# Second norm of an adaLN block: statistics and roots ahead of rests, and the second layer's first weight sums and splits issued sooner

## The chip, the cores and the metric

The kernel runs on one core of a Trainium2 chip. A core has five engines, each with an instruction queue of its own that it works through in order: TensorE (PE; its weight loads are listed as PEld), VectorE (DVE), ScalarE (ACT), GpSimd (POOL) and SyncE (SP), which issues most DMA transfers. They meet only through semaphores. SBUF is the working memory, PSUM the memory that TensorE writes its results to. The metric is the device time of one execution in microseconds (us), the median of several runs.

## The reference

The reference is one block of a network on 2048 tokens x 640 channels, fp32, with two halves that are modulated by a condition vector `c`:

```
mod = silu(c) @ w_mod                        # six rows of 640: sa, ca, ga, sb, cb, gb
h = layernorm(x) * (1 + ca) + sa             # x is A_q
x = x + ga * A(h, k, v, shift_k, ssm_k, ssm_D)   # short conv on k, times v, long FFT conv, gate by h
h = layernorm(x) * (1 + cb) + sb
x = x + gb * B(h, w1, b1, w2, b2)
# B: h2 = layernorm(h) over channels (2048 x 640)
#    u = gelu(h2^T w1 + b1)   (640 x 1728; the sum runs over the 2048 tokens)
#    y = u w2 + b2            (640 x 2048), returned as 2048 x 640
```

Between the halves stand two layernorms in a row: the one of the block ("first norm", its result times 1 + cb plus sb) and the one inside B ("second norm"). The change touches the stretch in which they are computed, and the beginning of the product with w2 ("second layer").

## The kernel before, in words

Tokens lie in 16 row blocks j = 0 to 15 of 128 tokens x 640 channels. Every fp32 product is made of three matmuls of a reduced fp32 form: a weight is split into a high part (a rounded copy, made by ScalarE) and a low part (the difference, made by VectorE), the data into a "half" (high) and a "rest" (low), and high x high, high x low and low x high are added in PSUM.

The long convolution of the first half ends with `gate` and the statistics of the new x. Then the program, written out by hand in one fixed order for all engines, works through the row blocks in **pairs** (pair pr holds blocks 2 pr and 2 pr + 1), each pair passing these steps:

- `x1_stats` (VectorE): a piece of statistics and their aggregation for each block; they are made for a pair some passes ahead.
- `root_in(n)`: one or two small POOL operations (lines 737 and 740) that add the epsilon to the variances of the second norm of one pair (their sums come from ScalarE's squares) and of the first norm of a later pair (from `x1_stats`), then ScalarE's square root (line 741). `root(n)` (VectorE) makes the reciprocal roots from them, in a Newton step of four small operations and a fifth for the first norm.
- `norm1` (ScalarE, line 755): the first norm of a pair. `second` (VectorE, lines 761 to 766): the modulation, with the sum for the mean of the second norm, and the subtraction of the mean; ScalarE squares the result (line 771) with a running sum.
- `halves` (ScalarE, line 775): the normalized block, rounded. `rests` (VectorE, line 779): what the rounding left.
- `products`: the matmuls of the pair with the first four blocks of w1 (f = 0 to 3), 48 in number, accumulated in four PSUM banks `acc[0..3]` over all pairs. Of a pair, 32 need the halves and the low parts of the weights, and 16 the rests. For the last pair, 7, they go block by block.
- `split_rows(r, ...)`: the split of the w1 rows of pairs 2 r and 2 r + 1 for these four blocks: four high parts on ScalarE (line 420) and four low parts on VectorE.

The loop over pr = 3 to 7 (second, rests of the pair before, products of the pair before, and so on) stands at the end of this stretch. Roots n = pr + 1 belong to the second norm of pair pr, since the lists in `roots` are one ahead; `root(pr + 1)` has to come before `halves(pr)`, and `rests(pr)` follows in the next pass. `load_w(4)`, in SP's queue, reloads the tile X once its rows have been split.

When the last pair's first block of products is done, the tile of the first weight block is free, `split_w(4)` fills it, and `u_evac` applies gelu to `acc[0..3]`; then come the other blocks of w1 (line 445), a half block (line 919) and the first four columns of w2 (line 1123), kept in `acc[0..3]` again.

The other 12 columns of w2 are multiplied by a scheme that needs seven products instead of eight for a 2 x 2 arrangement of blocks (line 1046). Six pairs p of columns, seven products each, make products n = 0 to 41, in the order A11, A12, S1, S2, S3, S4, A22; S1 to S4 are sums and differences of weight blocks, made by VectorE in `sums(n)`: S1 in sums(2), S2 and S3 in sums(3), S4 in sums(5), all others empty; so for every pair. `split(n)` makes the high part on ScalarE (line 1034) and the low part on VectorE, in one of three slots, n % 3, so that it has to wait for product(n - 3). `product(n)` is 21 matmuls. `outcome(n)` reads its result from PSUM; where an output block is complete, `finish` adds the bias, multiplies by the gate row, adds x and starts the transfer out. Products 0 and 1 share a PSUM tile, and so do 2 and 3; product 4 takes the bank of `acc[2]`, product 5 that of `acc[3]`, which hold columns 2 and 3 of w2 until four calls of `finish` (k = 0 to 3) have read them. `x_pair` loads the x rows for the finishes of a pair of columns.

Of the kernel before, what the change touches and what calls it, by code (L numbers as in the profile page):

```python
# [47 lines left out]
def mixer_kernel(ctx: ExitStack, tc: tile.TileContext, q, k, v, shift_k, ssm_k, ssm_D, w1, b1, w2, b2, c,  # L48
# [11 lines left out]
    def mem(tag, n, name=None):  # L60

        return sb.tile([128, n], F32, name=name or tag, tag=tag, bufs=1)
# [14 lines left out]
    T_in, P, X, T_aux, T_kt = mem("in", 4288), mem("p", 2048), mem("x", 2048), mem("aux", 4096), mem("kt", 1536)  # L77
# [339 lines left out]
    def split_rows(r, t, blocks, hi=True, lo=True):  # L417
        j, t = slice(4 * r, 4 * r + 4), t.rearrange("p (j m) -> p j m", j=4)
        for f in blocks if hi else ():
            act.activation(blk[f][0][:, j].bitcast(F32R), t[:, :, 128 * f:128 * f + 128], AF.Copy)  # L420
        for f in blocks if lo else ():
            TT(dve, blk[f][1][:, j].bitcast(F32R), t[:, :, 128 * f:128 * f + 128], blk[f][0][:, j], ALU.subtract)
# [291 lines left out]
    def x1_stats(js):  # L714
        for j in js:
            x1s(NC - 1, j)()
            dve.bn_aggr(mv[:, j, :], bst[:, j])
# [14 lines left out]
    def root_in(n):  # L732

        second_, first_ = roots[n]
        o = start[n]
        if second_:
            pool.tensor_scalar(V_[:, o:o + 2], V_[:, o:o + 2], 1 / D, EPS, op0=ALU.mult, op1=ALU.add)
            o += 2
        if first_:
            pool.tensor_scalar(V_[:, o:start[n + 1]], mv[:, first_[0]:first_[-1] + 1, 1], EPS, None, op0=ALU.add)  # L740
        act.activation(T_[:, start[n]:start[n + 1]], V_[:, start[n]:start[n + 1]], AF.Sqrt)

    def root(n):

        o = slice(start[n], start[n + 1])
        newton(R_[:, o], T_[:, o], V_[:, o])
        first_ = roots[n][1]
        if first_:
            f = slice(first_[0], first_[-1] + 1)
            dve.scalar_tensor_tensor(nm1[:, f], mv[:, f, 0], -1.0, R_[:, start[n + 1] - len(first_):start[n + 1]],  # L750
                                     op0=ALU.mult, op1=ALU.mult)
# [5 lines left out]
    def second(pr):  # L757

        for j in (2 * pr, 2 * pr + 1):
            t = row(j)  # L760
            dve.scalar_tensor_tensor(t, t, 1.0, CB, op0=ALU.mult, op1=ALU.mult, accum_out=su[:, j:j + 1])
        n = su[:, 2 * pr:2 * pr + 2]
        dve.tensor_scalar(n, n, msb, -1 / D, op0=ALU.add, op1=ALU.mult)
        for j in (2 * pr, 2 * pr + 1):
            t = row(j)
            dve.scalar_tensor_tensor(t, t, su[:, j:j + 1], SB, op0=ALU.add, op1=ALU.add)
        for j in (2 * pr, 2 * pr + 1):
            if j == 12:
                H.extend(unit(mem("xa", 5120, "h_x"), 4))
            H[j] = H[j][:, 0:640], H[j][:, 640:1280]  # L770
            act.activation(H[j][1].bitcast(F32R), row(j), AF.Square, accum_out=at(V_, 2, j))

    def halves(pr):
        for j in (2 * pr, 2 * pr + 1):
            act.activation(H[j][0].bitcast(F32R), row(j), AF.Identity, scale=at(R_, 2, j))

    def rests(pr):
        for j in (2 * pr, 2 * pr + 1):
            dve.scalar_tensor_tensor(H[j][1].bitcast(F32R), row(j), at(R_, 2, j), H[j][0], op0=ALU.mult,
                                     op1=ALU.subtract)  # L780

    def products(pr, fs=range(4)):
        for f_ in fs:
            if f_ == len(acc):
                acc.append(psum().rearrange("p (h m) -> p h m", h=2))
        js = [(f_, j) for j in (2 * pr, 2 * pr + 1) for f_ in fs]
        if pr == 7:
            for f_, j in sorted(js):
                mm(acc[f_], blk[f_][0][:, j], blk[f_][1][:, j], *H[j], False, j == 15)
            return  # L790
        for rest in range(2):
            for f_, j in js:
                wh, wl = blk[f_][0][:, j], blk[f_][1][:, j]
                mm(acc[f_], wh, wl, *H[j], j == 0 and not rest, False, ((wh, H[j][1]),) if rest else
                   ((wh, H[j][0]), (wl, H[j][0])))
# [47 lines left out]
    products(2)  # L843
    for pr in range(3, 8):
        second(pr)
        if pr > 3:
            rests(pr - 1)
            products(pr - 1)
        if pr in (4, 6):
            split_rows(pr // 2, X if pr == 4 else P, range(4), False, True)  # L850
        if pr < 6:
            x1_stats(range(2 * pr + 4, 2 * pr + 6))
        root_in(pr + 1)
        root(pr + 1)
        halves(pr)
        if pr < 6:
            norm1(pr + 2)
        if pr in (3, 5):
            split_rows(pr // 2 + 1, X if pr == 3 else P, range(4), True, False)
        if pr == 4:  # L860
            load_w(4)
    rests(7)
# [148 lines left out]
    def sums(n):  # L1011

        p, w_ = n // 7, ORDER[n % 7]
        if p >= NP:
            return
        a = lambda k: A[p, k]
        if w_ == "S1":
            A[p, w_] = S1
            TT(dve, S1, a("A21"), a("A22"), ALU.add)
        elif w_ == "S2":  # L1020
            TT(dve, a("A21"), a("A11"), a("A21"), ALU.subtract)
            TT(dve, a("A11"), S1, a("A11"), ALU.subtract)
            A[p, "S3"], A[p, "S2"] = a("A21"), a("A11")
        elif w_ == "S4":
            TT(dve, a("A12"), a("A12"), a("S2"), ALU.subtract)
            A[p, "S4"] = a("A12")

    def split(n):

        p, w_ = n // 7, ORDER[n % 7]  # L1030
        if p >= NP:
            return
        W[n] = slots[n % 3]
        act.activation(W[n][0].bitcast(F32R), A[p, w_], AF.Copy)  # L1034
        TT(dve, W[n][1].bitcast(F32R), A[p, w_], W[n][0], ALU.subtract)
# [24 lines left out]
    def outcome(n):  # L1060

        p, w_ = n // 7, ORDER[n % 7]
        t, s, x = bank.pop(n), NW + 2 * p, xq[4 * (p % 2):4 * (p % 2) + 4]
        if w_ == "A11":
            act.activation(p1, t, AF.Copy)
        elif w_ == "S1":
            act.activation(p5, t, AF.Copy)
        elif w_ == "A12":
            finish(s, 0, t, o1, x[0], p1)
        elif w_ == "S2":  # L1070
            TT(dve, u2, t, p1, ALU.add)
        elif w_ == "S3":
            TT(dve, u3, t, u2, ALU.add)
            TT(dve, u2, u2, p5, ALU.add)
            finish(s + 1, 1, u3, o4, x[3], p5)
            if p == NP - 1:
                TT(dve, u3, u3, GB[:, 0:320], ALU.mult)
                TT(dve, u3, u3, x[2], ALU.add)
        elif w_ == "S4":
            finish(s, 1, t, o2, x[1], u2)  # L1080
        elif p == NP - 1:
            finish(s + 1, 0, t, o3, u3)
        else:
            finish(s + 1, 0, t, o3, x[2], u3)
# [16 lines left out]
    for s in range(NW):  # L1101
        i = NF + s
        acc.append(psum().rearrange("p (h m) -> p h m", h=2))
        split_w(i)
        load_w(i + 1)
        if s < 3:
            t_ops(3 + s)
        if s > 1:
            early(s - 2)
        if s == 3:  # L1110
            load_pair(1, 0, 3)
            m_w.append(mem("w1", 4096, "m_w0"))
            slots += [(q7(m_w[0], 1792 * i), q7(m_w[0], 1792 * i + 896)) for i in range(2)]
            split(0)
            split(1)
            sums(2)
            sums(3)
        wh, wl = blk[i]
        for f_ in range(NF):
            u = U[f_]  # L1120
            for k, (w, r) in enumerate(((wh, 0), (wh, 2), (wl, 0))):
                for h in range(2):
                    pe.matmul(acc[s][:, h, 0:320], w[:, f_].bitcast(F32R), u[r + h].bitcast(F32R),  # L1123
                              start=f_ == 0 and k == 0, stop=f_ == NF - 1 and k == 2)
# [9 lines left out]
    t_ops(6, pool)  # L1134
    load_pair(1, 3, 4)
    for n in range(7 * NP):
        if n:
            sums(n + 3)
        split(n + 2)
        product(n)  # L1140
        if n == 1 or n == 3:
            outcome(n - 1)
        if n != 0 and n != 2:
            outcome(n)
        if n == 1:
            for k in range(4):
                finish(2 + k // 2, k % 2, acc[2 + k // 2][:, k % 2, 0:320], (o2, o4, o3, o1)[k], xq[4 + k])
        if n == 2:
            x_pair(1)
        if n % 7 == 6:  # L1150
            load_pair(n // 7 + 2)
            x_pair(n // 7 + 2)
# [34 lines left out]
```

## Time and profile before

| | |
|---|---|
| Time, three runs | 678.05, 681.95, 681.57 us (median 681.57) |
| Profiled execution | 683.93 us, span from first to last instruction 682.1 us |
| Mean granted TensorE clock over the span | 0.975 |
| Busy share of the span | PE 92%, PEld 88%, DVE 73%, ACT 44%, POOL 20% |
| VectorE's waits in the pair loop | ahead of the roots, 0.32 to 0.69 us each |

How to read it: a busy time counts every moment in which the engine had an instruction under way, so a busy TensorE need not be at its peak; matmuls of one shape follow each other in half of the duration that a row gives for one. In a row of a timeline stand the start, the duration of the group, the engine, the line of the program, the operation, output and inputs by the program's names, the shapes, the count, and in brackets the idle time ahead of it with what ended it. In a group of several instructions the duration runs from the first start to the last end. Instructions of VectorE and ScalarE overlap by some 0.08 us, so the distance of two starts is a little less than a duration. L57 is the line of a helper for elementwise operations of two tensors. The granted clock is the share of TensorE's full clock that it was given.

### The profile page before, as it was taken

To read this page: it belongs to the slowest core of one execution; us is meant where nothing else is said; L and a number is where in the kernel's file an instruction comes from. 1 tells how busy PE (TensorE), PEld (TensorE's weight loads), DVE (VectorE), ACT (ScalarE), POOL (GpSimd) and SP (SyncE) were. 2 spreads that over 40 slices of the span, in tenths; PEclk is the share of its full clock that TensorE was granted. 3 is DMA by queue.
4 is the path that set the end of the run, shared out by engine and by line. 5 is a ranking of instruction groups with operands and counts; after the bars stand their busy time and mean duration, and the time that the engine had idled before them with its cause. 6 is when DMAs were issued, how large, how long until landed. Compare 5 with 4: busy or idle time off the path is not lost.

```text
span 682.1 us, 20757 instructions
## 1 busy us (share of the span) xinstructions
PE 629.4 (92%) x9119; PEld 598.4 (88%) x9119; DVE 498.3 (73%) x869; ACT 300.2 (44%) x483; POOL 133.9 (20%) x157
## 2 busy tenths in 40 slices
PE   6878778999999898798899999999999989999997
PEld 2877568899989897688899889999999989999997
DVE  7789589989898279798866622321689779888995
ACT  1654655646657265457654222322344133333331
POOL 6762067226134142000000000000000520000000
PEclk9998989999999799888899999999999999999999
DMA  9999797375426153440308333335441634355601
GB/s 188 219 260 274 246 179 157 91 138 121 66 65 215 35 134 104 91 97 1 62 1 154 62 63 63 62 64 115 120 136 55 197 114 124 102 167 166 184 32 38
DMA packets 166538, 81.23 MB, mean 119 GB/s; under 512 B 90830, under 2 KB 156912, under 8 KB 166448
## 3 DMA queue, kind: packets, MB, share of 16 engines
q1 hardware_dynamic: 159276, 78.32, 47.5%
q10 hardware_dynamic: 6916, 1.31, 1.1%
q8 instruction: 71, 1.16, 0.7%
q0 software_dynamic: 256, 0.28, 0.2%
q14 instruction: 19, 0.16, 0.1%
HBM read 69.40 MB, written 10.49 MB: 117 GB/s over the span
## 4 chain that ended last, share of the span: by engine, by line
PE 68%; DVE 14%; ACT 6%; DMA 5%; issue 3%; SPq 2%; POOL 1%; ACTq 0%; POOLq 0%; DVEq 0%
PE pst L445 20%; PE pst L1046 17%; PE pst L1123 7%; PE pst L223 7%; PE pst L242 6%; PE pst L271 5%; PE pst L291 3%; DVE p L57 3%; ACT z L280 2%; DMA in<-in_w_mod_dram 1%; PE pst L919 1%; DVE tap L57 1%; DMA y<-in_A_ssm_k_dram 1%; DVE sm L548 1%; DVE kt L57 1%
## 5 line engine op out<-in xcount | busy, mean ns | idle before, releaser
L242 PE MATMUL pst<-z,w 128*64 128x64 f32 x2560 | 78.4, 223 | 13.1 <-DVE p L57 6.7
L242 PEld LDWEIGHTS pst<-z,w 128*64 128x64 f32 x2560 | 76.4, 138 | 15.6 <-issue 9.1
L229 ACT ACTIVATE z<-pst 128x1024 f32<-128x1024 f32 (+2 forms) x45 | 43.1, 977 | 46.3 <-PE pst L223 46.2
L57 POOL TENSOR_TENSOR y<-p 128x256 f32<-128x256 f32 x72 | 51.3, 741 | 42.4 <-DVE p L57 42.1
L57 DVE TENSOR_TENSOR p<-pst,kt 128x512 f32<-128x512 f32 x80 | 50.7, 680 | 7.9 <-ACT kt L246 7.9
L1046 PE MATMUL pst<-r_z,m_w 128*128 128x320 f32 x222 | 42.0, 312 | 2.2 <-DVE m_w L57 2.2
L882 ACT ACTIVATE pst<-pst,sm 128x640 f32<-128x640 f32 x13 | 10.0, 767 | 75.9 <-PE pst L445 75.9
L271 PEld LDWEIGHTS pst<-v,y 32*128 32x128 f32 x1280 | 38.2, 187 | 5.4 <-issue 4.8
L271 PE MATMUL pst<-v,y 32*128 32x64 f32 x1280 | 40.1, 272 | 2.5 <-issue 2.3
L246 ACT ACTIVATE kt<-pst 128x512 f32<-128x512 f32 x40 | 24.0, 599 | 34.6 <-PE pst L242 18.7
L1034 ACT ACTIVATE m_w<-m_v 128x896 fp32r<-128x896 f32 x24 | 22.7, 951 | 36.9 <-PE pst L1046 16.8
L223 PE MATMUL pst<-v,x 128*64 128x128 f32 x512 | 34.6, 291 | 4.5 <-issue 4.0
L223 PE MATMUL pst<-v,p 128*64 128x128 f32 x640 | 36.7, 274 | 0.8 <-ACT p L168 0.8
L1046 PEld LDWEIGHTS pst<-r_z,m_w 128*128 128x128 f32 x222 | 35.2, 190 | 2.4 <-DVE m_w L57 2.4
L57 POOL TENSOR_TENSOR m_p<-u_i,r_z 128x320 f32<-128x320 f32 x1 | 0.9, 875 | 183.4 <-issue 183.4
L223 PEld LDWEIGHTS pst<-v,p 128*64 128x64 f32 x640 | 34.8, 137 | 2.1 <-ACT p L168 1.7
L57 DVE TENSOR_TENSOR tap<-tap,kt 128x512 f32<-128x512 f32 x51 | 35.5, 696 | 1.3
L223 PEld LDWEIGHTS pst<-v,x 128*64 128x64 f32 x512 | 31.1, 147 | 5.8 <-issue 5.2
L291 PEld LDWEIGHTS pst<-z,v 64*64 64x64 f32 x1280 | 23.9, 156 | 9.1 <-issue 3.8
L280 ACT ACTIVATE z<-pst 128x512 f32<-128x512 f32 x38 | 20.9, 647 | 23.3 <-PE pst L271 23.3
L291 PE MATMUL pst<-z,v 64*64 64x64 f32 x1280 | 25.3, 241 | 6.3 <-issue 2.4
L57 DVE TENSOR_TENSOR kt<-in,tap 128x512 f32<-128x512 f32 x42 | 28.8, 685 | 1.2
(308 smaller groups left out, 1507.4 us busy)
## 6 DMA issues: line engine op xcount, KB each, us to landing
x<-in_B_w_dram SPq DMA_DIRECT2D x20, 512.0 KB
m_x<-xs SPq DMA_DIRECT2D x28, 160.0 KB
out_dram<-m_x SPq DMA_DIRECT2D x28, 160.0 KB
aux<-in_A_ssm_k_dram SPq DMA_DIRECT2D x8, 512.0 KB
m_v<-in_B_w_dram SPq DMA_DIRECT2D x9, 448.0 KB
in<-in_w_mod_dram SPq DMA_DIRECT2D x4, 960.0 KB
x<-in_B_w_dram SPq DMA_DIRECT2D x7, 448.0 KB
in<-in_A_v_dram SPq DMA_DIRECT2D x22, 128.0 KB
```

The source lines that it names most:

```text
L57: TT = lambda eng, o, a, b, op: eng.tensor_tensor(o, a, b, op=op)
L223: pe.matmul(ps[64 * ri:64 * ri + 64, o:o + 255:2], lhs, F1[:, 128 * ri:128 * ri + 128], start=True, stop=True)
L229: act.activation(Z[:, side, t, :, k0:k1], ps.rearrange("p (a k e) -> p a k e", a=4, e=2)[:, :, k0:k1], AF.Copy)
L242: pe.matmul(ps[64 * h:64 * h + 64, o:o + 64], W2[k1 // 32][:, 2 * (k1 % 32) + ri], rhs, start=True, stop=True)
L246: act.activation(kt.rearrange("p (m i) -> p m i", i=32), pv[:, :, 1], AF.Copy)
L271: pe.matmul(pp[qd // 2][:, o:o + 64], Y[p, ri, i:i + 2].rearrange("p i k -> p (i k)"), V2[p, 64 * ri:64 * ri + 64], start=ri == 0, stop=ri ...
L280: act.activation(o, i, AF.Copy)
L291: pe.matmul(ps[64 * b:64 * b + 64, 512 * e + 64 * jj:512 * e + 64 * jj + 64], V1[p, ri, n2], T2[p, :, 32 * ri + n2], start=ri == 0, stop=r ...
L445: pe.matmul(ps[0:m, h, 0:320], w_.bitcast(F32R), r_[:, 320 * h:320 * h + 320].bitcast(F32R), start=first and i == 0, stop=last and i == 2)
L1034: act.activation(W[n][0].bitcast(F32R), A[p, w_], AF.Copy)
L1046: pe.matmul(bank[n], w[:, i].bitcast(F32R), r.bitcast(F32R), start=i == 0 and k == 0, stop=i == 6 and k == 2)
L1123: pe.matmul(acc[s][:, h, 0:320], w[:, f_].bitcast(F32R), u[r + h].bitcast(F32R), start=f_ == 0 and k == 0, stop=f_ == NF - 1 and k == 2)
```

## The change

In the pair loop, `x1_stats` and `root_in(pr + 1)` stand right behind `second(pr)`, ahead of `rests(pr - 1)` and its products; before, the rests came first. The split of the w1 rows r = 2 and r = 3 is done as a whole in passes 4 and 6: its high parts stand between `root_in` and `root` (before, at the end of passes 3 and 5), its low parts behind the root, the halves and `norm1` (before, behind the products, ahead of the statistics).

In the second layer, sums(5) (S4 of the first pair) is issued ahead of all fast products, split(4) behind outcome(0) and ahead of outcome(1), split(5) behind product(2), and the four finishes are parted: two behind outcome(1), two behind split(5). From n = 4 on the order is as before.

```diff
     for pr in range(3, 8):
         second(pr)
+        if pr < 6:
+            x1_stats(range(2 * pr + 4, 2 * pr + 6))
+        root_in(pr + 1)
         if pr > 3:
             rests(pr - 1)
             products(pr - 1)
         if pr in (4, 6):
-            split_rows(pr // 2, X if pr == 4 else P, range(4), False, True)
-        if pr < 6:
-            x1_stats(range(2 * pr + 4, 2 * pr + 6))
-        root_in(pr + 1)
+            split_rows(pr // 2, X if pr == 4 else P, range(4), True, False)
         root(pr + 1)
         halves(pr)
         if pr < 6:
             norm1(pr + 2)
-        if pr in (3, 5):
-            split_rows(pr // 2 + 1, X if pr == 3 else P, range(4), True, False)
+        if pr in (4, 6):
+            split_rows(pr // 2, X if pr == 4 else P, range(4), False, True)
         if pr == 4:
             load_w(4)
...
             split(0)
             split(1)
-            sums(2)
-            sums(3)
+            for n in (2, 3, 5):
+                sums(n)
...
     for n in range(7 * NP):
-        if n:
+        if n > 2:
             sums(n + 3)
-        split(n + 2)
+        if n not in (2, 3):
+            split(n + 2)
         product(n)
         if n == 1 or n == 3:
             outcome(n - 1)
+        if n == 1:
+            split(4)
         if n != 0 and n != 2:
             outcome(n)
-        if n == 1:
-            for k in range(4):
+        if n == 2:
+            split(5)
+        if n in (1, 2):
+            for k in (2 * n - 2, 2 * n - 1):
                 finish(2 + k // 2, k % 2, acc[2 + k // 2][:, k % 2, 0:320], (o2, o4, o3, o1)[k], xq[4 + k])
         if n == 2:
             x_pair(1)
```

## The prediction

> **What bounds the kernel now.** I read the page first, then the chain that ended last, then the orders of the engines around the two places that the diff touches: the second norm (about 310 to 359 us) and the start of the second layer's fast products (about 541 to 577 us). The page says that TensorE is the bound on the whole, and that VectorE is the second engine of the chain:
>
> ```profile
> span 682.1 us, 20757 instructions
> ...
> PE 629.4 (92%) x9119; PEld 598.4 (88%) x9119; DVE 498.3 (73%) x869; ACT 300.2 (44%) x483; POOL 133.9 (20%) x157
> ...
> PE 68%; DVE 14%; ACT 6%; DMA 5%; issue 3%; SPq 2%; POOL 1%; ACTq 0%; POOLq 0%; DVEq 0%
> ```
>
> A change is therefore worth what it takes from TensorE's idle time, and from the half clock that follows such idle time. The price of one matmul comes from the longest piece of the chain, 98.75/672 = 0.147 us at full clock:
>
> ```profile
> 396.52 98.75 PE pst L445 x672
> ```
>
> TensorE's order shows what it waits for in the second norm (rows of line 445):
>
> ```profile
> 317.62 7.25 PE L445 MATMUL pst<-h_a,wb 128*128 128x320 f32 x48
> 327.62 4.09 PE L445 MATMUL pst<-h_a,wb 128*128 128x320 f32 x16 [2.75 <-ACT h_a L775]
> ...
> 344.10 14.34 PE L445 MATMUL pst<-h_x,wb 128*128 128x320 f32 x96 [0.61 <-ACT h_x L775]
> ```
>
> The 48 matmuls of products(3) end at 324.87; products(4) wait 2.75 us for halves(4), products(6) 0.61 us for halves(6). At the start of the second layer's fast part:
>
> ```profile
> 553.66 1.04 PE L1046 MATMUL pst<-r_z,m_w 128*128 128x320 f32 x6
> ...
> 556.74 0.45 PE L1046 MATMUL pst<-r_z,m_w 128*128 128x320 f32 x2
> 559.36 0.43 PE L1046 MATMUL pst<-r_z,m_w 128*128 128x320 f32 x1 [2.17 <-DVE m_w L57]
> ...
> 569.96 1.04 PE L1046 MATMUL pst<-u_t,m_w 128*128 128x320 f32 x6
> ```
>
> product(3) runs from 553.66, product(4) from 556.74 does two matmuls with its high parts and then waits 2.17 us for VectorE's low part; product(7) begins at 569.96. The windows give the clock right behind that wait and later:
>
> ```profile
> 561.00:562.00 1.00, 1.00 (x6) 1.00 (x5) 0.89 (x1) 0.00 (x0) 0.00 (x0) 0.50 0.29 100
> ...
> 570.00:575.00 5.00, 5.00 (x36) 5.00 (x36) 4.90 (x8) 1.60 (x3) 0.00 (x0) 1.00 0.28 87
> ```
>
> The column behind the five engines is the granted clock: 0.50, then 1.00. Products 4 to 6 are 63 matmuls, 63 x 0.147 = 9.26 us; they took 569.96 - 556.74 = 13.22. So 3.96 us are lost here: 2.17 of waiting and 1.79 of half clock.
>
> **Part B, the second layer's first sums and splits (the larger part).** VectorE's order there, and ScalarE's two high splits:
>
> ```profile
> 540.01 1.65 DVE L57 TENSOR_TENSOR m_v<-m_p,m_v 128x896 f32<-128x896 f32 x1
> 548.91 1.24 DVE L57 TENSOR_TENSOR m_w<-m_p,m_w 128x896 fp32r<-128x896 f32 x1 [7.26 <-ACT m_w L1034]
> 550.08 1.76 DVE L57 TENSOR_TENSOR m_w<-m_v,m_w 128x896 fp32r<-128x896 f32 x1
> 551.76 0.54 DVE L1055 SCALAR_TENSOR_TENSOR m_x<-pst,sm,m_x 128x320 f32<-128x320 f32 x1
> ...
> 553.27 0.55 DVE L1053 SCALAR_TENSOR_TENSOR m_x<-pst,sm,rows 128x320 f32<-128x320 f32 x1
> ...
> 557.22 1.08 DVE L57 TENSOR_TENSOR m_v<-m_v 128x896 f32<-128x896 f32 x1
> 558.22 2.27 DVE L57 TENSOR_TENSOR m_w<-m_v,m_w 128x896 fp32r<-128x896 f32 x2
> ...
> 564.00 0.49 DVE L57 TENSOR_TENSOR m_x<-pst,m_x 128x320 f32<-128x320 f32 x1 [2.11 <-PE pst L1046]
> ...
> 574.61 1.08 DVE L57 TENSOR_TENSOR m_w<-m_p,m_w 128x896 fp32r<-128x896 f32 x1
> ```
> ```profile
> 551.12 0.94 ACT L1034 ACTIVATE m_w<-m_v 128x896 fp32r<-128x896 f32 x1
> 558.42 0.95 ACT L1034 ACTIVATE m_w<-m_v 128x896 fp32r<-128x896 f32 x1 [6.36 <-DVE m_v L57]
> ```
>
> Before, split(4)'s low part (558.22) stands behind outcome(1) (551.76 to 553.27, 1.51 us), four finishes (553.27 to 557.22, 3.95 us, 0.99 each) and sums(5) (557.22, 1.08).
>
> - sums(5) moves into the idle stretch of 7.26 us that ends at 548.91. It costs 1.08 to 1.65 us there (the row at 540.01 is the same operation, slowed) and nothing on the path; its cover is wide.
> - split(4)'s low part can start once split(3)'s has ended (550.08 + 1.76 = 551.84) and its high part is there (551.12 + 0.94 = 552.06): 552.1 to 553.1. product(4) then finds it 3.6 us ahead of 556.74, so the 2.17 go, and with the idle time the half clock, 1.79.
> - What is late next? VectorE goes on with outcome(1) to 554.6, two finishes to 556.6, split(5)'s low part to 557.6 (its high part is free once product(2) has left its slot, at 553.66), two finishes to 559.6, outcome(3)'s 0.4 and split(6)'s 1.0 to 561.0. product(4) needs the bank of acc[2], read by the first two finishes until about 556.2; product(5), at 559.83, that of acc[3], read until 559.2. So 0.6 us of margin is the least so far.
> - From outcome(4) to the start of split(9)'s low part VectorE took 574.61 - 564.00 = 10.61 us without a gap; from 561.0 it is there at 571.6 and done at 572.7. TensorE, five products of 3.09 after 556.74, begins product(9) at 572.2 and wants the low part in its third matmul, 572.5. It waits 0.2 us. Later pairs give VectorE time to catch up.
> - The output and x transfers keep their order in SP's queue. The four x loads of the next pair leave up to 2.4 us later, with the last two finishes (559.6, not 557.2); they are used by outcome(8), past 573. Cost nothing.
>
> Part B: 3.96 - 0.2 = 3.75 us. Bounds: 1.9 if the half clock would stay (2.17 - 0.2), 4.0 if nothing waits.
>
> **Part A, the second norm.** VectorE's order in the pair loop (second at 316.73, rests 320.21, low splits 321.80, statistics 324.21, root 325.87, and so on):
>
> ```profile
> 316.73 0.82 DVE L761 SCALAR_TENSOR_TENSOR xb<-xb,kt 128x640 f32<-128x640 f32 x1
> ...
> 320.21 1.67 DVE L779 SCALAR_TENSOR_TENSOR h_a<-xa,kt,h_a 128x640 fp32r<-128x640 f32 x2
> 321.80 2.49 DVE L57 TENSOR_TENSOR wb<-x,wb 128x512 fp32r<-128x512 f32 x4
> 324.21 0.28 DVE L548 BATCH_NORM_STATS2 sm<-xb 128x6 f32<-128x128 f32 x1
> ...
> 325.87 0.18 DVE L326 RECIPROCAL kt<-kt 128x4 f32<-128x4 f32 x1 [0.57 <-ACT kt L741]
> ...
> 333.55 0.18 DVE L326 RECIPROCAL kt<-kt 128x4 f32<-128x4 f32 x1 [0.57 <-ACT kt L741]
> ...
> 334.49 0.82 DVE L761 SCALAR_TENSOR_TENSOR xb<-xb,kt 128x640 f32<-128x640 f32 x1
> ...
> 342.37 0.17 DVE L326 RECIPROCAL kt<-kt 128x2 f32<-128x2 f32 x1 [0.32 <-ACT kt L741]
> ...
> 348.57 0.17 DVE L326 RECIPROCAL kt<-kt 128x2 f32<-128x2 f32 x1 [0.32 <-ACT kt L741]
> ...
> 350.30 1.68 DVE L779 SCALAR_TENSOR_TENSOR h_x<-xb,kt,h_x 128x640 fp32r<-128x640 f32 x2 [0.90 <-ACT h_x L775]
> ```
>
> From starts: second 3.48, rests 1.59 (1.67 to the end), low splits 2.41, statistics 1.09 (324.21 to 325.30, where the 0.57 of idle time begin), root 0.94. Nothing is added or removed; the order changes, and the one thing to win on VectorE is the wait ahead of a root: 0.57 behind statistics, 0.32 behind rests or splits. The root's inputs pass POOL, and POOL shows how it fares beside VectorE:
>
> ```profile
> 315.02 0.19 POOL L737 TENSOR_SCALAR kt<-kt 128x2 f32<-128x2 f32 x1 [8.14 <-ACT h_a L771]
> ...
> 323.44 0.90 POOL L737 TENSOR_SCALAR kt<-kt 128x2 f32<-128x2 f32 x1 [7.93 <-ACT r_z L771]
> ...
> 347.61 0.70 POOL L737 TENSOR_SCALAR kt<-kt 128x2 f32<-128x2 f32 x1 [5.51 <-ACT h_x L771]
> ```
>
> Beside statistics it takes 0.19. Begun in the third of four low splits (323.44; they start 0.6 apart from 321.80) it ends at 324.34, just behind the fourth (321.80 + 2.49 = 324.29); begun during a pair of rests (347.61) it takes 0.70 and ends at 348.31, 0.26 ahead of the root at 348.57. The new order puts rests right behind the statistics, so POOL's second small operation, or both, wait until the rests end, and the root comes 0.32 (one held) or 0.62 (both held) after them.
>
> The Trainium skill, "SBUF — State Buffer", section "Who interferes with whom", has this: a VectorE instruction with two SBUF inputs and a GpSimd instruction that reads SBUF exclude each other, for the whole instruction. It speaks against the new order. Taken at its word POOL would come in between the two rests, the 0.32 would vanish from two roots, and the sum would be some 0.6 higher; the row at 323.44, held past the end of the third split, says that it does not come in between.
>
> Step by step, with one held / both held: pass 4 has second at 316.73, statistics from 320.21, rests(3) from 321.30 to 322.97, root at 323.29 / 323.59 (before: 325.87), low splits behind it, second(5) at 326.64 / 326.94 against 325.87 + 0.94 = 326.81. Pass 5: 3.48 + 1.09 + 1.67 = 6.24, and 0.32 / 0.62, against 333.55 - 326.81 = 6.74. Passes 6 and 7 hold the same operations with the same 0.32. So VectorE ends its chain 0.35 us sooner to 0.25 later; I take 0.05, as each of the two waits is near a tie.
>
> For TensorE the halves count. ScalarE's operations:
>
> ```profile
> 319.74 2.18 ACT L420 ACTIVATE wb<-x 128x512 fp32r<-128x512 f32 x4
> ...
> 326.74 0.83 ACT L775 ACTIVATE h_a<-xb,kt 128x640 fp32r<-128x640 f32 x1 [0.91 <-DVE kt L329]
> ```
>
> Root(5)'s square root ends about 323.3 to 323.6, the four high splits now stand behind it (2.1), then halves(4), whose first is done at 326.2 to 326.5: products(4) start 1.1 to 1.4 sooner. By the same steps products(6) start about 342.5, not 344.10. But products(7) also need rests(7), which end VectorE's chain at 350.30 + 1.68 = 351.98. Before, TensorE came to products(7) at 344.10 + 48 x 0.149 = 351.2, when the first rest was just there (351.14). Now it comes sooner and waits: its first block ends ten matmuls after the first rest, 351.14 + 1.47 = 352.6, less VectorE's gain, against 351.2 + 12 x 0.147 = 353.0. The last 36 matmuls, the first weight split and the first gelu all hang on that block and move with it.
>
> Part A: 0.4 + 0.05 = 0.45 us (0.15 to 0.75). load_w(4), in SP's queue behind the low splits, leaves some 2.4 us later, with over 20 us to its use: nothing.
>
> **Sum.** 3.75 + 0.45 = 4.2 us. The profiled execution took 683.93 us (its span and 1.83 around it) and would take 679.7; it lies 2.36 above the median of the three runs, 681.57, from which the forecast is 681.57 - 4.2 = **677.4 us**. The runs lie between 678.05 and 681.95, so the gain is about their spread; 1% is about what a measurement of this kernel can tell from no change.
>
> **The rivals.**
> - *The half clock was this execution's alone.* Idle of 2.75 and 2.17 us was followed by half clock, idle of 0.61 was not; a wait of 2.17 may cost the clock only in some executions. Then part B is worth 2.17 - 0.2, the sum 2.4, the time 679.2. For it: the runs differ by 3.9 us. Against: the windows show it. The Trainium skill, "TensorE: Matmul & The Clock Gate", Part 1, says that the clock is set by a free-running window of about 3.4 us of activity; by that rule this rival holds in a part of the executions. Chance 0.22.
> - *The norm gains nothing:* both POOL operations are held and halves win nothing at the end. Part B alone: 677.8. Chance 0.12.
> - *Slower.* VectorE's queue at the second layer: the last two finishes, which free product(5)'s bank, now stand behind split(5)'s low part. If its high part came only after product(4) (559.83 + 0.95 = 560.8), the low part would end at 561.8, the bank be free at 563.4, and product(5) wait 3.6 us and lose 1.8 more to the clock: 5.4 lost for 3.96 won, with part A 1.0 slower, 682.6. It decides from a wait of 2.6 us on. For it: before, that high part ran at 558.42, behind product(3). Against: the row puts that wait to VectorE's sums(5), which is gone. Chance 0.04.
> - *More:* the executions to come lie where the fastest of the three did, 678.05 - 4.2 = 673.9. Chance 0.12.
>
> The forecast itself has 0.50, 676 to 679. Leaving out the slower case and half of the last, and with 2 us above the first rival for the spread of the runs, the range is 673.6 to 681.2. Faster by over 1% means below 674.8: most of the last case and a little of the forecast, 0.14; slower by over 1%: 0.03; within: 0.83.
>
> **What would show it.** Right: no TensorE wait for VectorE near 557, products 4 to 9 at 3.09 us each at clock 1.00, split(4)'s low part ahead of outcome(1). In the norm: high splits between square root and halves, POOL's operations held until the rests end, a wait of about 0.3 to 0.6 ahead of each root still there, and TensorE waiting for the last rests. Wrong: a new wait of over 1 us at product(5) or product(9), half clock between 553 and 573, or a VectorE chain in the norm that is shorter by over 1 us.

## The result and the profile after

The changed kernel takes 677.97 us (median of 20 runs, 676.58 to 684.35), the kernel before 681.7 us (20 runs, 677.66 to 685.6); the ratio is 0.9955, 95% interval 0.9935 to 0.9974, so it is faster by 0.26 to 0.65%. The forecast was 677.4 us, in the case "within 1%". The profiled execution took 679.75 us against 683.93 before: 4.18 us less, where the sum said 4.2. The page of the changed kernel:

```profile
span 678.0 us, 20758 instructions
...
PE 629.8 (93%) x9119; PEld 596.7 (88%) x9119; DVE 499.0 (74%) x869; ACT 300.4 (44%) x483; POOL 134.7 (20%) x157
```

The span is 4.1 us shorter at nearly the same busy times. That the two spans differ by nearly what the two stages below gained is luck in part: second(0), where the norm begins, starts at 282.43 us in the one execution and at 282.55 in the other, while in the traces of all kernels here it starts anywhere between 279.1 and 285.7.

**The second layer.** TensorE's order in the kernel before, the start of product(0):

```profile
544.42 1.04 PE L1046 MATMUL pst<-u_t,m_w 128*128 128x320 f32 x6
```

and in the changed kernel, the starts of products 0, 7 and 14 (the rows that read `u_t`) and of product(9):

```profile
543.87 1.04 PE L1046 MATMUL pst<-u_t,m_w 128*128 128x320 f32 x6
...
565.42 1.04 PE L1046 MATMUL pst<-u_t,m_w 128*128 128x320 f32 x6
...
571.59 1.43 PE L1046 MATMUL pst<-r_z,m_w 128*128 128x320 f32 x6
...
587.37 1.04 PE L1046 MATMUL pst<-u_t,m_w 128*128 128x320 f32 x6
```

The first seven products took 569.96 - 544.42 = 25.54 us before and 565.42 - 543.87 = 21.55 now: 3.99 us less. No row of TensorE's order in these seven has a wait in brackets any more. The next seven take 21.95; six matmuls of product(9) last 1.43 us where the other groups of six last 1.04, which is a new wait of 0.39 inside product(9). The weight loads show what it waits for:

```profile
572.15 0.59 PEld L1046 LDWEIGHTS pst<-r_z,m_w 128*128 128x128 f32 x4 [0.38 <-DVE m_w L57]
```

The windows of the changed kernel have full clock (1.00 behind the five engines) where before had 0.50:

```profile
556.00:560.00 4.00, 4.00 (x30) 4.00 (x28) 3.93 (x8) 1.96 (x3) 0.00 (x0) 1.00 0.34 125
```

VectorE's order in the changed kernel shows how:

```profile
541.14 1.09 DVE L57 TENSOR_TENSOR m_v<-m_v 128x896 f32<-128x896 f32 x1
548.36 1.25 DVE L57 TENSOR_TENSOR m_w<-m_p,m_w 128x896 fp32r<-128x896 f32 x1 [6.13 <-ACT m_w L1034]
...
551.53 1.09 DVE L57 TENSOR_TENSOR m_w<-m_v,m_w 128x896 fp32r<-128x896 f32 x1 [0.24 <-ACT m_w L1034]
...
558.02 0.55 DVE L1053 SCALAR_TENSOR_TENSOR m_x<-pst,sm,rows 128x320 f32<-128x320 f32 x1
...
571.01 1.08 DVE L57 TENSOR_TENSOR m_w<-m_p,m_w 128x896 fp32r<-128x896 f32 x1
```

sums(5) is the row at 541.14, inside the former idle stretch; split(4)'s low part stands at 551.53, ahead of outcome(1); the last finish reads its bank until 558.57; split(9)'s low part is at 571.01 to 572.09.

**The second norm.** As a measure I take the time from the first operation of second(0) on VectorE to the fifth block of w1 on TensorE. Before:

```profile
282.43 0.83 DVE L761 SCALAR_TENSOR_TENSOR t_g<-t_g,kt 128x640 f32<-128x640 f32 x1
...
359.33 2.91 PE L445 MATMUL pst<-r_z,wb0b 128*128 128x320 f32 x18 [0.89 <-DVE u_x L57]
```

After, with TensorE's waits in between:

```profile
282.55 0.83 DVE L761 SCALAR_TENSOR_TENSOR t_g<-t_g,kt 128x640 f32<-128x640 f32 x1
```
```profile
326.13 2.61 PE L445 MATMUL pst<-h_a,wb 128*128 128x320 f32 x16 [1.14 <-ACT h_a L775]
...
332.06 1.44 PE L445 MATMUL pst<-h_a,wb 128*128 128x320 f32 x8 [0.96 <-DVE h_a L779]
...
350.87 7.01 PE L445 MATMUL pst<-h_x,wb 128*128 128x320 f32 x46 [0.36 <-DVE h_x L779]
...
358.78 2.90 PE L445 MATMUL pst<-r_z,wb0b 128*128 128x320 f32 x18 [0.90 <-DVE u_x L57]
```

76.90 us before, 76.23 after: 0.67 us. Products(4) start 1.6 us sooner (43.58 behind second(0), not 45.19), but TensorE then waits for the rests, 0.96 us inside products(4) and 0.36 inside products(7), and these are VectorE's. Its roots in the changed kernel:

```profile
323.31 0.18 DVE L326 RECIPROCAL kt<-kt 128x4 f32<-128x4 f32 x1 [0.35 <-ACT kt L741]
...
333.14 0.18 DVE L326 RECIPROCAL kt<-kt 128x4 f32<-128x4 f32 x1 [0.35 <-ACT kt L741]
...
348.21 0.17 DVE L326 RECIPROCAL kt<-kt 128x2 f32<-128x2 f32 x1 [0.32 <-ACT kt L741]
...
349.93 1.68 DVE L779 SCALAR_TENSOR_TENSOR h_x<-xb,kt,h_x 128x640 fp32r<-128x640 f32 x2 [0.90 <-ACT h_x L775]
```

Counted from second(0), root(5) comes 2.68 us sooner (the low splits now stand behind it), root(6) 0.53 and root(8) 0.48. What stays is a wait of 0.32 to 0.35 ahead of each of these roots, 5 to 8; the roots ahead of them wait as before. POOL's and VectorE's rows in pass 5 show what goes on there:

```profile
331.20 0.85 POOL L737 TENSOR_SCALAR kt<-kt 128x2 f32<-128x2 f32 x1 [8.16 <-ACT r_z L771]
332.13 0.74 POOL L740 TENSOR_SCALAR kt<-sm 128x2 f32<-128x2 f32 x1
```
```profile
331.19 0.82 DVE L779 SCALAR_TENSOR_TENSOR h_a<-xb,kt,h_a 128x640 fp32r<-128x640 f32 x1
331.92 0.88 DVE L779 SCALAR_TENSOR_TENSOR r_z<-xb,kt,r_z 128x640 fp32r<-128x640 f32 x1
```

POOL's first operation ends (332.05) just behind the first rest (332.01), its second (332.87) just behind the second rest (332.80). Beside statistics such operations take 0.19 and 0.22 us (at 315.02 and 325.38 of before). At these lengths both would be done about 1.2 us sooner, by 331.7, and the square root ahead of the second rest's end. That is an estimate; by it the wait comes from POOL being held, not from the way over POOL as such.

### The profile page after: what moved, and what is told of

It reads as the page before. It is cut to its first block, busy times and chain, and to the rows that moved or that the text cites. A ratio compares the mean times of both kernels' runs of the same rounds, so it can differ in the third digit from the quotient of the medians.

```text
span 678.0 us, 20758 instructions
## 1 busy us (share of the span) xinstructions
PE 629.8 (93%) x9119; PEld 596.7 (88%) x9119; DVE 499.0 (74%) x869; ACT 300.4 (44%) x483; POOL 134.7 (20%) x157
## 3 DMA queue, kind: packets, MB, share of 16 engines
q8 instruction: 71, 1.16, 0.7%
## 5 line engine op out<-in xcount | busy, mean ns | idle before, releaser
L242 PE MATMUL pst<-z,w 128*64 128x64 f32 x2560 | 80.2, 225 | 12.0 <-DVE p L57 6.0
L242 PEld LDWEIGHTS pst<-z,w 128*64 128x64 f32 x2560 | 78.2, 140 | 14.6 <-issue 8.5
L291 PEld LDWEIGHTS pst<-z,v 64*64 64x64 f32 x1280 | 25.3, 164 | 8.9 <-issue 3.6
L291 PE MATMUL pst<-z,v 64*64 64x64 f32 x1280 | 26.8, 249 | 6.2 <-ACT g L369 2.3
L57 DVE TENSOR_TENSOR m_w<-m_v,m_w 128x896 fp32r<-128x896 f32 x24 | 27.9, 1165 | 2.5 <-ACT m_w L1034 2.1
```

Of the source, the lines that this page charges most:

```text
L57: TT = lambda eng, o, a, b, op: eng.tensor_tensor(o, a, b, op=op)
L242: pe.matmul(ps[64 * h:64 * h + 64, o:o + 64], W2[k1 // 32][:, 2 * (k1 % 32) + ri], rhs, start=True, stop=True)
L291: pe.matmul(ps[64 * b:64 * b + 64, 512 * e + 64 * jj:512 * e + 64 * jj + 64], V1[p, ri, n2], T2[p, :, 32 * ri + n2], start=ri == 0, stop=r ...
```

## The experiments

**The two parts alone.** First the norm: the changed pair loop in the kernel before, without the hunks for `sums`, `split` and `finish`.

> The pair loop of the changed kernel, the second layer as before. My theory (VectorE's chain through the rests bounds the norm's end, its root waits only shrink from 0.57 to 0.35 us): the first block of w1 behind the norm starts 0.5 to 0.8 us sooner counted from root(3), the whole gains 0.4 to 0.8 us, which a measurement hardly tells from nothing; the second layer still shows a wait of about 2.2 us at product(4). Rival (TensorE's sooner start bounds it): 1.1 to 1.4 us or more. For the clock: the windows behind the 2.2 us wait show half clock again if it follows from the length of the wait alone; full clock if it depends on where the wait falls.

Measured: ratio to before 0.9993 (0.9966 to 1.002), 682.28 us. Its trace, with the window behind the wait:

```profile
280.22 0.83 DVE L761 SCALAR_TENSOR_TENSOR t_g<-t_g,kt 128x640 f32<-128x640 f32 x1
```
```profile
356.47 2.90 PE L445 MATMUL pst<-r_z,wb0b 128*128 128x320 f32 x18 [0.90 <-DVE u_x L57]
```
```profile
556.49 0.42 PE L1046 MATMUL pst<-r_z,m_w 128*128 128x320 f32 x1 [2.16 <-DVE m_w L57]
```
```profile
558.00:560.00 2.00, 2.00 (x10) 2.00 (x9) 1.03 (x2) 0.00 (x0) 0.00 (x0) 0.50 0.19 67
```

The stretch is 76.25 us as in the changed kernel: the norm's part is worth 0.65 us, too little for the measured times to tell from nothing. The second layer's wait of 2.16 us and the half clock behind it are there again, in a second execution.

Then the second layer: the hunks for `sums`, `split` and `finish` alone.

> The second layer's part alone, the pair loop as before. My theory: no wait at product(4), products 4 to 8 at 3.08 us each, 0.4 us of wait at product(9); gain 3.1 to 3.8 us, nearly the whole of the change (the median of 20 runs gave 3.7 for both parts). Rival (the half clock behind the wait was one execution's alone): about 2 us. The pair loop shows a wait of 2.7 us ahead of products(4) as before, and the windows behind it tell whether half clock follows it in this execution too.

Measured: ratio 0.9944 (0.9915 to 0.9973), 679.11 us. In its trace the first seven products take 21.56 us and the next seven 21.96, a gain of 3.6 us in the stages, as expected; the interval of the ratio, some 1.8 to 5.8 us, does not exclude the rival's 2. There is half clock behind the 2.77 us wait ahead of products(4) that the old pair loop keeps:

```profile
326.00:329.00 3.00, 3.00 (x11) 3.00 (x12) 2.93 (x6) 3.00 (x6) 0.00 (x0) 0.50 1.19 204
```

**One half of the second layer's part.** In the kernel before, only this:

```diff
-            sums(2)
-            sums(3)
+            for n in (2, 3, 5):
+                sums(n)
...
-        if n:
+        if n and n != 2:
             sums(n + 3)
```

> Before, with sums(5) alone moved ahead of the fast products; split(4) stays behind outcome(1) and the four finishes. My theory: TensorE's wait at product(4) shrinks from 2.17 to about 1.1 us, too short to be followed by half clock, so that the gain is 1.1 and most of the 1.8 of the clock: 2.0 to 2.9 us. Rival (the clock falls behind any wait of about a us, or the clock has no part): 1.1 us.

Measured: ratio 0.9969 (0.9940 to 0.9998), 680.32 us. The trace:

```profile
545.29 1.04 PE L1046 MATMUL pst<-u_t,m_w 128*128 128x320 f32 x6
...
559.22 0.41 PE L1046 MATMUL pst<-r_z,m_w 128*128 128x320 f32 x1 [1.16 <-DVE m_w L57]
...
568.27 1.04 PE L1046 MATMUL pst<-u_t,m_w 128*128 128x320 f32 x6
```
```profile
559.00:563.00 4.00, 3.78 (x26) 3.78 (x27) 3.23 (x6) 0.92 (x2) 0.00 (x0) 1.00 0.67 207
```

The wait is 1.16 us, 1.01 less, and no half clock follows in this execution; seven products take 22.98 us, 2.56 less than before. So 1.08 us of VectorE's work moved out of the way brought 2.56 us, as the theory said: more than half of it is the clock. This rests on one trace; the interval of the ratio, some 0.1 to 4.1 us, cannot tell it from the rival's 1.1. Moving the two splits and the finishes as well brings the other 1.4.

**The changed kernel again**, beside its parts:

> The changed kernel once more on the same chip as its parts. If the parts add up: its gain is that of the norm alone plus that of the second layer alone, 3.7 to 4.4 us, ratio 0.9935 to 0.9955. In its trace the 2.5 us wait ahead of products(2) stands as before; half clock behind it in one execution and not in another would show that the clock depends on where the wait falls.

Ratio 0.9947 (0.9922 to 0.9972), 678.32 us; its norm takes 76.23 us and its first seven products 21.56. The parts add up in the stages (0.67 + 3.98 of the first seven products - 0.39 in product(9)); by the ratios the two parts alone make 0.9937, which lies in both intervals that the changed kernel has so far.

**What is left ahead of the roots.** In the changed kernel, ScalarE takes the root from the raw numbers, and POOL's operations come behind:

```diff
         if second_:
+            act.activation(T_[:, o:o + 2], V_[:, o:o + 2], AF.Sqrt, scale=1 / D, bias=epsc)
             pool.tensor_scalar(V_[:, o:o + 2], V_[:, o:o + 2], 1 / D, EPS, op0=ALU.mult, op1=ALU.add)
             o += 2
         if first_:
+            act.activation(T_[:, o:start[n + 1]], mv[:, first_[0]:first_[-1] + 1, 1], AF.Sqrt, bias=epsc)
             pool.tensor_scalar(V_[:, o:start[n + 1]], mv[:, first_[0]:first_[-1] + 1, 1], EPS, None, op0=ALU.add)
-        act.activation(T_[:, start[n]:start[n + 1]], V_[:, start[n]:start[n + 1]], AF.Sqrt)
```

> The changed kernel, with the square roots taken by ScalarE straight from the sums and variances (scale and epsilon in the activation), so that POOL's small operations stand beside the way to the root and are needed only by its third operation. My theory (VectorE's chain bounds the norm's end, and what is left of its waits ahead of the roots, 0.35, 0.35, 0.32 and 0.32 us, is POOL held by the rests): these four waits fall to under 0.1 us, that of root(4) from 0.69 to about 0.15, and from the start of products(2) to that of the fifth block of w1 it takes 48.0 to 48.5 us, not 49.7; total 1.2 to 1.8 us under the changed kernel, ratio to before about 0.992. Rival (the waits are ScalarE's own way, squares and square root, whoever adds the epsilon): they stay above 0.25 us and the time does not move.

Measured: ratio 0.9872 (0.9841 to 0.9903), 676.37 us. The trace:

```profile
285.70 0.82 DVE L762 SCALAR_TENSOR_TENSOR t_g<-t_g,kt 128x640 f32<-128x640 f32 x1
...
324.92 0.17 DVE L326 RECIPROCAL kt<-kt 128x4 f32<-128x4 f32 x1
```
```profile
359.12 2.91 PE L445 MATMUL pst<-r_z,wb0b 128*128 128x320 f32 x18 [0.89 <-DVE u_x L57]
```

No wait stands ahead of root(5) any more (nor of 6, 7 and 8), and the stretch is 73.42 us, 2.8 less than in the changed kernel: all eight roots and not four gained, 0.2 to 0.4 each. From the start of products(2), as the expectation measured it, it takes 47.7 us, a little less than the 48.0 to 48.5 expected. So the waits ahead of roots 5 to 8 were POOL's, and the rival, ScalarE's own way, is out for these. It is not out for roots 1 to 4, which have no rests right ahead of them: there 0.28 to 0.46 us stay, with ScalarE named, and root(4) was a miss with 0.40 where about 0.15 was expected:

```profile
317.95 0.18 DVE L326 RECIPROCAL kt<-kt 128x4 f32<-128x4 f32 x1 [0.40 <-ACT kt L741]
```

The profiled execution took 680.10 us, no less than the changed kernel's 679.75, because its norm starts at 285.70 us and not at 282.55. The gain over the changed kernel is seen in the stage, not in that execution's total; and the ratio, below the 0.992 expected, comes from six runs.

**Who bounds the norm.** In the changed kernel, `split_rows(..., True, False)` behind `halves(pr)` instead of ahead of `root(pr + 1)`:

> The changed kernel with the high weight splits behind the halves instead of ahead of them. TensorE gets halves(4) and halves(6) sooner by about 1 us each, but VectorE's low splits wait for the high ones, some 2 us in each of the passes 4 and 6. My theory (VectorE's chain bounds): products(4) start about 1 us sooner and the fifth block of w1 all the same 3 to 4 us later, 53 us after products(2), not 49.7. Rival (what TensorE waits for there bounds): the fifth block starts about 1 us sooner.

Measured: ratio 0.9985 (0.9961 to 1.0009), 682.09 us, so most of the change's gain is lost. TensorE's and VectorE's rows:

```profile
325.58 0.56 PE L445 MATMUL pst<-h_a,wb 128*128 128x320 f32 x2 [1.30 <-ACT wb L420]
```
```profile
281.84 0.83 DVE L761 SCALAR_TENSOR_TENSOR t_g<-t_g,kt 128x640 f32<-128x640 f32 x1
...
325.56 2.50 DVE L57 TENSOR_TENSOR wb<-x,wb 128x512 fp32r<-128x512 f32 x4 [1.94 <-ACT wb L420]
...
343.79 2.50 DVE L57 TENSOR_TENSOR wb<-p,wb 128x512 fp32r<-128x512 f32 x4 [2.14 <-ACT wb L420]
```
```profile
362.23 2.03 PE L445 MATMUL pst<-r_z,wb0b 128*128 128x320 f32 x12 [0.89 <-DVE u_x L57]
```

One expectation was a miss: products(4) do not start sooner (43.74 behind second(0), not 43.58), for they need the weights' high parts as well as the halves. The end came out nearly as expected (53.9 us behind the start of products(2), not 53): VectorE waits 1.94 + 2.14 = 4.08 us for the high parts, and the stretch is 80.39 us, 4.16 longer. VectorE's chain passes its delay on whole.

**Both, and the wait in product(9).** c_root_without_pool with outcome(6) behind split(9); beside the hunk above, the edit is:

```diff
-        if n != 0 and n != 2:
+        if n == 7:
+            outcome(6)
+            x_pair(2)
+        if n not in (0, 2, 6):
             outcome(n)
...
-            x_pair(n // 7 + 2)
+            if n > 6:
+                x_pair(n // 7 + 2)
```

> c_root_without_pool and, in the second layer, outcome(6) behind split(9) instead of ahead of sums(10), with the x loads of the third pair behind it. My theory: the wait of 0.4 us inside product(9) goes too, since VectorE comes to split(9) 1.5 us sooner; 0.4 us below c_root_without_pool, 1.6 to 2.2 below the changed kernel. Rival (another wait takes its place in the products after it): the time of c_root_without_pool.

Measured: ratio 0.9896 (0.9869 to 0.9923), 676.69 us, not told apart from c_root_without_pool. The same kernel and the changed one were then timed on one chip:

> The kernel of f_root_and_late_outcome once more, now on the same chip as the changed kernel. By the lengths of the stages in the traces so far (norm 2.8 us shorter than the changed kernel's at full clock, 2.1 with half clock in it, second layer 0.4) it lies 2.5 to 3.2 us below the changed kernel. If the clock takes part of that back in most executions: under 2 us.

> The changed kernel beside it: ratio to before 0.994 to 0.996. Its norm and second layer have the lengths of the two traces of it so far (76.2 us from the first second() to the fifth block, 21.6 and 22.0 us for the first two pairs), wherever the half clock falls ahead of them.

Ratios to before 0.9893 (0.9840 to 0.9946) and 0.9928 (0.9898 to 0.9957), medians 674.18 and 676.95 us. The ratio of the changed kernel lies just below the 0.994 to 0.996 expected; its stages are those expected (76.23 us for the norm, 21.56 and 21.93 for the first two groups of seven products). The trace of the former:

```profile
279.12 0.82 DVE L762 SCALAR_TENSOR_TENSOR t_g<-t_g,kt 128x640 f32<-128x640 f32 x1
```
```profile
353.26 2.92 PE L445 MATMUL pst<-r_z,wb0b 128*128 128x320 f32 x18 [0.89 <-DVE u_x L57]
...
559.91 1.04 PE L1047 MATMUL pst<-u_t,m_w 128*128 128x320 f32 x6
...
581.48 1.04 PE L1047 MATMUL pst<-u_t,m_w 128*128 128x320 f32 x6
```

The second seven products take 21.57 us, so the 0.39 are gone. The norm takes 74.13 and 74.14 us in the two traces of this kernel, not 73.42: in both a stretch of half clock fell behind the wait of 1.88 us for the rests of products(4), 0.55 in this window of f_root_and_late_outcome:

```profile
330.00:333.70 3.70, 3.70 (x17) 3.70 (x17) 3.42 (x12) 2.59 (x4) 0.40 (x1) 0.55 0.26 45
```

In c_root_without_pool the same wait of 1.88 us had full clock behind it. So the half clock does cost 0.7 us there, since with VectorE 2.8 us sooner TensorE has little slack left. In the stages this kernel stands 2.5 us below the changed kernel; in the medians 2.8, with intervals that overlap. c_root_without_pool's interval lies below that of the changed kernel in all but one of its three timings (0.9935 to 0.9974, 0.9922 to 0.9972, 0.9898 to 0.9957); the ratios were taken on different chips, so this is a sign and no proof.

**The bank of product(5).** In the changed kernel, finishes k = 2 and 3 and `x_pair(1)` behind split(6), at n = 4.

> The changed kernel with the last two finishes, which free the bank of product(5), behind split(6) instead of split(5). By the prediction's rival for slower the bank decides: VectorE reads it until about 560.2 by the changed kernel's trace, where product(5) started at 559.26, so that TensorE waits about 1 us there; too short for half clock; cost 0.5 to 1.1 us. If the bank does not bind: no wait and the time of the changed kernel.

Measured: ratio 0.9936 (0.9905 to 0.9967), 679.01 us. The trace:

```profile
560.45 1.56 PE L1046 MATMUL pst<-u_i,m_w 128*128 128x320 f32 x9 [0.96 <-ACT m_w L1034]
```
```profile
559.76 0.54 DVE L1053 SCALAR_TENSOR_TENSOR m_x<-pst,sm,rows 128x320 f32<-128x320 f32 x1
```

A wait of 0.96 us, and from product(0) to product(7) 22.76 us, not 21.55. The view names ScalarE's split, done at 554.18 in this trace; the last finish reads its bank until 560.30, and product(5) starts at 560.45. With only the finishes and the x loads moved, the wait is for the bank that the finishes read. In this trace product(9) no longer waits, so the net cost is 0.8 us by the stages, in the expected range; the ratio is not told apart from the changed kernel's.

## Why the prediction was right, and where its steps were off

- **Part B, 3.75 us: measured 3.99 - 0.39 = 3.60.** The wait and the half clock went, sums(5) is covered, split(4)'s low part came within 0.1 us of the forecast place (551.53 is 552.1 less the 0.55 by which everything comes sooner). The margin at product(5)'s bank was 0.69 (0.6 forecast), and the experiment that moved the finishes turned it into a wait. The term that was mis-sized is product(9): 0.39 us, not 0.2. VectorE's low part ended where it was forecast (572.09 is 572.7 less about 0.6), but I had let TensorE want it at its third matmul; the weight load ahead of that matmul stood still from 571.77 on.
- **Part A, 0.45 us: measured 0.67.** Its limit was named rightly: TensorE starts sooner and then waits for VectorE's rests. The two terms were off in opposite ways: VectorE's chain gained 0.48, not 0.05, and TensorE's side of the last block the remaining 0.2, not 0.4. The step that failed is that of POOL. Both of its operations were held, which I had priced at 0.62 ahead of the root; but each was held by one rest, so only 0.35 followed. The row at 323.44 of before, held over the end of one instruction, had led me to say that POOL doesn't come in between two. The rule of the Trainium skill ("SBUF — State Buffer", "Who interferes with whom": for the whole instruction) describes the rests of the changed kernel better, and the trace agrees there (332.05 behind 332.01, 332.87 behind 332.80); what I made of it, that the 0.32 would vanish, does not hold, since the second POOL operation meets the second rest.
- **The rival of the half clock.** Behind the wait of 2.2 us at product(4) it was there in both executions that have this wait, so the full price was the right one for these. The runs cannot show it for each execution timed; the gain by the medians, 3.7, and by the ratio, 3.1 (1.8 to 4.4), leaves room for executions without it.
- **Norm gains nothing, slower:** the norm's gain of 0.65 to 0.7 us stands in the traces of the changed kernel and of a_norm_alone, and the bank's wait needed a further delay to appear.
- **The sum, 4.2 us: measured 3.60 + 0.67 = 4.27 in the stages, 3.7 in the medians.** That the stages come so near is luck in part: part B was forecast 0.15 too high and part A 0.22 too low.

## What to carry to other kernels

Price an idle stretch of TensorE with the clock behind it: here 2.2 us of waiting cost 4 in the traces, and shortening it to 1.2 brought 2.6 in one. When a short chain across engines (squares, POOL, root, reciprocal) stands ahead of an engine that is nearly always busy, look which hop shares something with that engine: taking POOL's hop off the path shortened the stage by three to four times as much as the reordering (2.1 or 2.8 us against 0.67). And before an operation is moved ahead for one consumer, list everything else that consumer needs: the halves alone did not start the products.

## What the runs showed that I had not expected

The half clock does not follow from the length of a wait alone. Ahead of products(2) stands a wait of 2.48 us in the kernel before and in the changed one; behind it before ran at half clock and the changed kernel at full clock:

```profile
311.00:313.00 2.00, 2.00 (x9) 2.00 (x9) 1.93 (x6) 1.85 (x3) 0.00 (x0) 0.50 0.00 0
```
```profile
311.00:313.00 2.00, 2.00 (x16) 2.00 (x15) 1.93 (x6) 1.99 (x3) 0.00 (x0) 1.00 0.00 0
```

The changed kernel alone shows the same. In i_after_beside, a third execution of it, the wait is 2.48 us again, and half clock follows:

```profile
305.74 8.85 PE L445 MATMUL pst<-r_v,wb 128*128 128x320 f32 x48 [2.48 <-ACT r_v L775]
```
```profile
308.00:310.00 2.00, 2.00 (x9) 2.00 (x9) 1.93 (x6) 1.66 (x3) 0.00 (x0) 0.50 0.00 0
```

So one program meets either clock behind one and the same wait. Of the eight traces with a wait of 2.47 or 2.48 us ahead of products(2), two have half clock behind it; of the three with 1.88 us inside products(4), two have. The experiment with the shorter wait at product(4) has to be read with this in mind: its one trace shows that half clock need not follow 1.16 us, and nothing about how often it would.

Ahead of products(2) the half clock cost nothing: b_layer_alone, with full clock at that place and the same old loop, takes the same 76.90 us, because VectorE bounds the stretch. The Trainium skill, "TensorE: Matmul & The Clock Gate", Part 1, says that the clock follows a free-running window of activity; the traces agree in that the same wait meets either clock. No run here shows the window itself.
